# Layer-norm statistics in one block, a planner with other durations, and sums formed by accumulating DMAs, in a gated long-convolution and token-mixing kernel

## The chip, the cores and the metric

The kernel runs on one core of one Trainium2 chip. The metric is the device time of one execution in microseconds (us), as a median of runs; below it stands beside the profile of one further execution, whose span goes from its first to its last instruction. The engines are called PE (matrix), DVE (vector), ACT (scalar), POOL (GpSimd) and SP (which here only issues DMAs).

## The reference, cut to what matters

Inputs are bf16; S is 2048 positions, D is 640 channels, F is 1536. Branch `a` is a causal convolution over the whole sequence, done by Fourier transforms of length 4096; branch `b` is a layer norm followed by an MLP along the sequence (not along the channels); a sigmoid gate per position mixes them.

```
x = A_q
g = sigmoid((x * gate_w).sum(-1, keepdims=True))
# branch a
kv = (4-tap causal shift convolution of A_k) * A_v
y  = irfft(rfft(kv, 2S) * rfft(ssm_k, 2S))[:S] + kv * ssm_D
a  = A_q * y
# branch b
h = layernorm(x)                         # over D
u = gelu(einsum("sd,sf->df", h, w1) + b1)
b = (einsum("df,fs->ds", u, w2) + b2).T
return g * a + (1 - g) * b
```

## The kernel before, in words

Everything of the computation lives in SBUF, 128 partitions wide; the positions are cut into four groups `hk` of 512, each of four tiles `p` of 128, so a tile number is t = 4 hk + p. The stages are these.

- **Loads.** SP issues nearly all of them; `ssm_k`, the rows of A_q into `X`, `k`, `v`, three column chunks of `w1` into two buffers `ring`, then `w2` in four pieces into two buffers `W2` that lie over `ring`.
- **Filter.** PE transposes `ssm_k` (`transp`, tile `wT`), multiplies it with a table of sines `FTB` (`fwd`, groups of four matmuls that ACT evicts into `C`), for two halves h; `mixing` on DVE turns four tile transforms into the spectrum; `v1mix` accumulates by two pairs of POOL DMAs. The filter's spectra are called V0 and V1.
- **Statistics.** `ln_tile` (L840) runs two bn_stats and one bn_aggr per tile on DVE; `ln_apply` (L849), called after every four tiles, forms 1/sqrt(var + eps) on POOL (a sum and a power on four columns) and normalises the four tiles of `X` in place on DVE. POOL also builds `KF`, the taps of the shift convolution, in two large products.
- **Shift convolution and forward transform of kv.** `k_turn` copies `k` into `kp` on DVE and transposes it by DMA into `KT`; `kv` (L897) multiplies with `KF` on PE, ACT evicts `ksh`, DVE multiplies with `v`. Then `fwd` and `mixing` as for the filter give the spectra A0 and A1 (halves of the sequence).
- **First MLP product (m1).** 12 blocks ft of 32 matmuls, X against `ring`, ACT applies gelu into `GT`. Its priority numbers are far above those of the other work, so it fills PE where nothing else is ready.
- **Gate.** DVE multiplies X with `gate_w` into three buffers `gq` that lie over `KF`; ACT sums each (`gsum`, output to `junk`).
- **Second MLP product (m2).** 16 tiles of 24 matmuls in the order of `HORD` (hk = 2, 3, 0, 1), GT against `W2`; ACT evicts into `O1` with bias and gate.
- **Spectral products** on DVE. `cross` (L1038) forms A0 V1 in place of V1, in four halves (two spectra, i = 0 and 1); `y1` (L1045) forms A1 V0 in place of A1 through the scratch `tm[0]` and `tm[1]` and adds `cross`'s result by POOL DMAs (`acc_dma`); `product` does A0 V0. A complex number is held as two blocks of 1280 columns per slot.
- **Inverse.** `invmix` on DVE undoes `mixing` (giving Z1 for the second half of the sequence, Z0 for the first); `inverse` (L1068) runs the inverse transforms on PE with the table `GTB` (DMA transposes of `FTB`), ACT evicts with the gate into one of three buffers `cgb`, DVE multiplies by q (`q_hi` or `q_lo`, loaded a second time) and adds to `O1`, and SP stores the result.

The order of all instructions is made by a planner in the kernel itself, `_Sched.run` (L382): each operation has a duration written down in the code, and a priority that is its number in program order unless one is given; a simulated clock goes forward, and each engine takes the ready operation with the lowest priority number. PSUM is four slots; the MLP may hold two of them and the other products three. The order so found is emitted for each engine, and on the chip each engine and each DMA queue keeps it: an operation whose input is late holds up all that is behind it. The durations are in `dve_dur`, `act_dur`, `mms` and in single calls. A DMA is planned at 0.1 us of issue, its bytes at a rate, and 2 us to landing. `_Tracker` finds the semaphore waits from the memory that each operation reads and writes, so a buffer placed over another (`at=base_of(...)`) brings waits with it.

Nearly all matmuls carry line 293 in the profile, tensor_tensor 617, tensor_scalar 627 and 628, ACT's work 655, copies of k 724, POOL's DMAs 262, SP's 267 and the DMA transposes 260.

Of the kernel before, what the change touches and what calls it, by code (L numbers as in the profile page):

```python
# [322 lines left out]
class _Sched:  # L323
# [58 lines left out]
    def run(self):  # L382
# [29 lines left out]
        while started < n:  # L412
# [6 lines left out]
            for e in engs:  # L419
# [32 lines left out]
                if e in ("SP", "QA") or op.lat < 0:  # L452
# [3 lines left out]
                    op.end = dma_free + 2.0  # L456
# [48 lines left out]
def _build(nc, A_q, A_k, A_v, A_shift_k, A_ssm_k, A_ssm_D, B_x, B_w1, B_b1, B_w2, B_b2, gate_w, out):  # L505
# [10 lines left out]
    with ExitStack() as es:  # L516
# [34 lines left out]
        gwb = alloc("gwb", [128, D], BF16)  # L551
        Drow = alloc("Drow", [1, D], BF16)
        ident = alloc("ident", [128, 128], BF16)
# [7 lines left out]
        vtmp = alloc("vtmp", [128, 16], F32)  # L561
# [21 lines left out]
        gq = [alloc(f"gq{i}", [128, 2, D], BF16, at=base_of(KF) + 2560 * i) for i in range(3)]  # L583
        junk = alloc("junk", [128, D], BF16, at=base_of(KF) + 7680)
# [14 lines left out]
        q_hi = alloc("q_hi", [128, 2, 4, D], BF16, at=base_of(C[0]))  # L599
# [67 lines left out]
        def mms(vt, items, prio=None, name="mm"):  # L667
            dur = sum(max(n_of(r) / 2400.0, 0.06) for _, _, r, _, _ in items)
# [51 lines left out]
        def k_turn(hk):  # L720
# [3 lines left out]
            SC.add("DVE", 0.85, lambda s: T.op("DVE", lambda e: e.tensor_copy(ov, iv), [i[:, :, :]], [o[:, :, :]]), [i[:, :, :]], [o[:, :, :]], prio=0, name="kperm")  # L724
# [115 lines left out]
        def ln_tile(hk, p):  # L840
            t = 4 * hk + p
            xs = X[:, hk, p, :]
            for ci in range(2):
                o, i = stats[:, t, 6 * ci:6 * ci + 6], xs[:, 320 * ci:320 * ci + 320]
                SC.add("DVE", 0.46, (lambda o, i: lambda s: T.op("DVE", lambda e: e.bn_stats(o, i), [i], [o]))(o, i), [i], [o])  # L845
            o, i = mv[:, t, :], stats[:, t, :]
            SC.add("DVE", 0.2, (lambda o, i: lambda s: T.op("DVE", lambda e: e.bn_aggr(o, i), [i], [o]))(o, i), [i], [o])

        def ln_apply(hk):  # L849
            r = slice(4 * hk, 4 * hk + 4)  # L850
            ts("POOL", vtmp[:, r], mv[:, r, 1], 1e-5, None, ALU.add)
            tt("POOL", rstd[:, r], vtmp[:, r], V(cst, 1, [[0, 4]]), ALU.pow)
            for p in range(4):
                t = 4 * hk + p
                ts("DVE", X[:, hk, p, :], X[:, hk, p, :], mv[:, t, 0:1], rstd[:, t:t + 1], ALU.subtract, ALU.mult, mode=4, extra=0.17)

        srcW = lambda h: (lambda kt, p, ci: wT[:, 2 * h + kt, p, 320 * ci:320 * ci + 320])
        for h in range(2):
# [5 lines left out]
            if h == 0:  # L864
                for hk in range(4):
                    for p in range(4):
                        ln_tile(hk, p)
                    ln_apply(hk)
# [63 lines left out]
        for ft in range(FT):  # L932
# [14 lines left out]
            if ft == 0:  # L947
                act(junk[:, :], gwb[:, :], ACT.Copy, acc=gws[:, :], name="gws").after.add(g_)
# [18 lines left out]
        def w2_load(hk):  # L967
            for a in range(2):
                dma(W2[hk % 2][:, 6 * a:6 * a + 6, :], dr(B_w2, a * 6 * 128 * S + 512 * hk, [[S, 128], [128 * S, 6], [1, 512]]), 128 * 6144)

# [3 lines left out]
        HORD = (2, 3, 0, 1)  # L974
        for n_, hk in enumerate(HORD):
            w2_load_at = n_
            W2h = W2[n_ % 2]
            for a in range(2):
                dma(W2h[:, 6 * a:6 * a + 6, :], dr(B_w2, a * 6 * 128 * S + 512 * hk, [[S, 128], [128 * S, 6], [1, 512]]), 128 * 6144)
# [57 lines left out]

        def cross(g):  # L1038
# [114 lines left out]
```

## Time and profile before

| | us |
|---|---|
| median of 3 runs (lowest to highest) | 198.19 (197.91 to 199.74) |
| the profiled execution, its own time | 197.93 |
| its span | 196.1 |
| PE busy | 177.4 |
| DVE busy | 177.0 |
| ACT busy | 118.5 |
| POOL busy | 28.6 |

The mean granted clock of PE was 0.996. In the rows of a timeline, the first number is the start in us from the start of the span, the second the time from the first start to the last end of the merged instructions, then engine, line, operation, output and inputs by the program's names (buffer numbers left out) and their number (x); in brackets stands how long the engine stood idle just before and what ended it. In the rows of groups, the numbers behind the bar are the busy time in us and the mean duration of one in ns, then the idle time before them. Starts of neighbouring instructions overlap a little with the ends of those before, so that the price of one in a row of its kind is read from start to start. PE's ends are modelled.

### The profile page before, as it was taken

The numbers are of one execution on the slowest core, as the hardware profiler recorded it, in microseconds if no ns is written. First come the engines' busy times: TensorE is split into PE (matmuls) and PEld (weight loads), VectorE is DVE, ScalarE is ACT, GpSimd is POOL, SyncE is SP. The second block draws the span as 40 slices with busy tenths as digits, with TensorE's granted clock in tenths as the row PEclk, the third lists the DMA queues.
The fourth block names the chain that finished last, engine by engine and source line by source line (L and its number), as shares of the span: only waits on it lengthen the run. The fifth ranks groups of instructions, "written<-read, shape, count | busy, mean of one in ns | idle before, by whom it ended". The sixth has DMA issues, their size and how long they took to land.

```text
span 196.1 us, 3370 instructions
## 1 busy us (share of the span) xinstructions
PE 177.4 (90%) x1403; PEld 131.4 (67%) x1403; DVE 177.0 (90%) x196; ACT 118.5 (60%) x187; POOL 28.6 (15%) x30
## 2 busy tenths in 40 slices
PE   0759987999999999999999999999999979997890
PEld 0546564468767787777777778888888867775560
DVE  7996998799999179999999879999999599989994
ACT  4798967997749793799796413131313117664471
POOL 2629802500005400000000000040400000000000
PEclk9999999999999999999999999999999999999998
DMA  5999999994999999960053008029999960222034
GB/s 162 331 409 379 364 209 253 310 417 143 165 276 265 227 199 191 258 202 0 3 185 135 3 24 282 15 64 232 234 305 231 383 269 5 91 76 101 3 107 160
DMA packets 36719, 37.62 MB, mean 192 GB/s; under 512 B 15579, under 2 KB 32608, under 8 KB 36704
## 3 DMA queue, kind: packets, MB, share of 16 engines
q1 hardware_dynamic: 34464, 32.15, 54.4%
q0 software_dynamic: 2176, 5.24, 14.4%
q8 instruction: 11, 0.18, 0.4%
q14 instruction: 4, 0.03, 0.0%
q10 hardware_dynamic: 64, 0.01, 0.0%
HBM read 25.87 MB, written 2.62 MB: 145 GB/s over the span
## 4 chain that ended last, share of the span: by engine, by line
PE 67%; DVE 16%; DMA 9%; ACT 3%; POOL 2%; issue 2%; SPq 0%; DVEq 0%
PE pp L293 67%; DMA kn<-in_A_k_dram 5%; DMA X<-in_A_q_dram 4%; DVE kp L724 3%; DVE stats L845 2%; DVE C L617 2%; DVE SS L617 2%; DVE X L628 2%; ACT ksh L655 2%; DVE vkv L617 1%; DVE cgb L617 1%; DVE O L617 1%; POOL rstd L617 1%; POOL vtmp L627 1%; ACT cgb L655 1%
## 5 line engine op out<-in xcount | busy, mean ns | idle before, releaser
L293 PE MATMUL pp<-X,ring 128*128 128x320 bf16 x384 | 55.5, 299 | 1.6 <-DVE X L628 1.6
L617 DVE TENSOR_TENSOR C<-C 128x2560 bf16<-128x2560 bf16 (+1 forms) x28 | 48.9, 1773 | 8.3 <-ACT C L655 5.5
L293 PE MATMUL pp<-GT,W 128*128 128x320 bf16 x384 | 52.8, 299 | 1.1 <-ACT O L655 1.1
L293 PEld LDWEIGHTS pp<-GT,W 128*128 128x128 bf16 x384 | 43.5, 113 | 10.0 <-issue 1.4
L293 PEld LDWEIGHTS pp<-X,ring 128*128 128x128 bf16 x384 | 36.6, 98 | 17.6 <-DVE X L628 2.0
L655 ACT ACTIVATE C<-pp 128x640 bf16<-128x640 f32 x64 | 39.9, 723 | 5.5 <-PE pp L293 5.2
L655 ACT ACTIVATE O<-pp,c,omg 128x640 bf16<-128x640 f32 (+1 forms) x17 | 14.5, 853 | 37.9 <-PE pp L293 37.9
L617 DVE TENSOR_TENSOR tm<-C,C 128x2560 bf16<-128x2560 bf16 (+1 forms) x12 | 22.8, 1930 | 0.0
L262 POOL DMA_DIRECT2D C<-C x6 | 7.5, 1406 | 90.1 <-DVE C L617 90.1
L293 PE MATMUL pp<-wT,FTB 128*128 128x320 bf16 x128 | 20.2, 314 | 0.4 <-ACT wT L655 0.4
L655 ACT ACTIVATE GT<-pp,cc 128x640 bf16<-128x640 f32 x12 | 9.5, 792 | 14.6 <-PE pp L293 14.5
L617 DVE TENSOR_TENSOR C<-tm 128x1280 bf16<-128x1280 bf16 (+1 forms) x16 | 18.0, 1154 | 0.1
L293 PEld LDWEIGHTS pp<-wT,FTB 128*128 128x128 bf16 x128 | 11.9, 102 | 7.8 <-ACT C L655 2.3
L655 ACT ACTIVATE cgb<-pp,gg 128x640 bf16<-128x640 f32 x16 | 12.6, 794 | 6.4 <-PE pp L293 3.3
L293 PE MATMUL pp<-C,GTB 128*128 128x320 bf16 x96 | 13.7, 299 | 2.2 <-DVE C L617 2.2
L293 PE MATMUL pp<-ident,ssm 128*128 128x128 bf16 x80 | 8.4, 265 | 6.2 <-DVE pint L617 5.3
L845 DVE BATCH_NORM_STATS2 stats<-X 128x6 f32<-128x320 bf16 x32 | 13.5, 460 | 0.4 <-DMA X<-in_A_q_dram 0.4
L293 PEld LDWEIGHTS pp<-C,GTB 128*128 128x128 bf16 x96 | 9.2, 98 | 6.4 <-DVE C L617 2.5
L655 ACT ACTIVATE junk<-gq 128x640 bf16<-128x640 bf16 x16 | 11.8, 737 | 0.5
L293 PEld LDWEIGHTS pp<-ident,ssm 128*128 128x128 bf16 x80 | 6.5, 127 | 8.0 <-DMA ssm<-in_A_ssm_k_dram 5.3
L655 ACT ACTIVATE wT<-pp 128x640 bf16<-128x640 f32 x16 | 10.2, 711 | 2.6 <-PE pp L293 2.6
L655 ACT ACTIVATE ksh<-pp 128x1024 bf16<-128x1024 f32 (+1 forms) x12 | 9.6, 893 | 3.2 <-PE pp L293 3.2
(63 smaller groups left out, 176.6 us busy)
## 6 DMA issues: line engine op xcount, KB each, us to landing
ring<-in_B_w_dram SPq DMA_DIRECT2D x12, 512.0 KB, 10.9
W<-in_B_w_dram SPq DMA_DIRECT2D x8, 768.0 KB, 6.9
C<-C POOLq DMA_DIRECT2D x6, 640.0 KB, 11.3
ssm<-in_A_ssm_k_dram SPq DMA_DIRECT2D x4, 640.0 KB, 9.0
X<-in_A_q_dram SPq DMA_DIRECT2D x4, 640.0 KB, 9.3
kn<-in_A_k_dram SPq DMA_DIRECT2D x4, 640.0 KB, 8.5
out_dram<-O SPq DMA_DIRECT2D x7, 320.0 KB, 2.3
vkv<-in_A_v_dram SPq DMA_DIRECT2D x2, 640.0 KB, 4.7
```

The costliest lines, as they stand in the source:

```text
L262: ins = engobj.dma_start(out_ap, in_ap, accum_op=ALU.add, max_dma_last_dim=2560)
L293: ins = self.nc.tensor.matmul(ps_ap, lhsT=lhsT, rhs=rhs, start=start, stop=stop, skip_group_check=True)
L617: return SC.add(eng, d, lambda s: T.op(eng, lambda e: e.tensor_tensor(o, a, b, op), [a, b], [o]), [a, b], [o], prio=prio, name="tt")
L627: return e.tensor_scalar(o, a, s1, None, op0=op0)
L628: return e.tensor_scalar(o, a, s1, s2, op0=op0, op1=op1)
L655: return T.op("ACT", lambda e: e.activation(o, src, func, **kw), rr + [src], ww)
L724: SC.add("DVE", 0.85, lambda s: T.op("DVE", lambda e: e.tensor_copy(ov, iv), [i[:, :, :]], [o[:, :, :]]), [i[:, :, :]], [o[:, :, :]], prio ...
L845: SC.add("DVE", 0.46, (lambda o, i: lambda s: T.op("DVE", lambda e: e.bn_stats(o, i), [i], [o]))(o, i), [i], [o])
```

## The change

1. The planner's durations are altered: DVE 0.04 or 0.08 us of fixed time in place of 0.1 or 0.16, ACT 0.09 + 0.05 per operand in place of 0.19 + 0.09, matmuls 2.5 ns more, bn_stats 0.38 for 0.46, bn_aggr 0.12 for 0.2, the k copy 0.75 for 0.85; a POOL DMA lands 3 us later.
2. `ln_apply` is called once, after all 16 tiles, on 16 columns; POOL also forms the root `sd`, which saves a DVE operation in the gate.
3. `cross`: of the two products that formed A0 V1's first block by a wide product and an add, each is a narrow product now; the second goes to a quarter of `tm[0]` and a POOL DMA adds it.
4. The epilogue of the second half (h = 1) adds to `O1` by a POOL DMA from `cgb`.
5. Memory: `q_hi` lies over `Drow` and `KF` (before over `C[0]`), `gq` over `GTB` (before over `KF`), `junk` is gone.
6. Order in the program: `q_hi` is loaded ahead of the `W2` loads, `q_lo` not before the last of them; the A0 products come behind the first inverse.

```diff
-                    op.end = dma_free + 2.0
+                    op.end = dma_free + 2.0 + (3.0 if e == "POOL" else 0.0)
...
-        gq = [alloc(f"gq{i}", [128, 2, D], BF16, at=base_of(KF) + 2560 * i) for i in range(3)]
-        junk = alloc("junk", [128, D], BF16, at=base_of(KF) + 7680)
+        gq = [alloc(f"gq{i}", [128, 2, D], BF16, at=base_of(GTB) + 2560 * i) for i in range(3)]
...
-        q_hi = alloc("q_hi", [128, 2, 4, D], BF16, at=base_of(C[0]))
+        q_hi = alloc("q_hi", [128, 2, 4, D], BF16, at=base_of(Drow))
...
-            return n / {1: 960.0, 2: 1920.0, 4: 3840.0}[mode] + (0.1 if mode == 4 else 0.16)
+            return n / {1: 960.0, 2: 1920.0, 4: 3840.0}[mode] + (0.04 if mode == 4 else 0.08)
...
-            return n / 1200.0 + 0.19 + 0.09 * nap
+            return n / 1200.0 + 0.09 + 0.05 * nap
...
-            dur = sum(max(n_of(r) / 2400.0, 0.06) for _, _, r, _, _ in items)
+            dur = sum(max(n_of(r) / 2400.0 + 0.0025, 0.056) for _, _, r, _, _ in items)
...
-        def ln_apply(hk):
-            r = slice(4 * hk, 4 * hk + 4)
-            ts("POOL", vtmp[:, r], mv[:, r, 1], 1e-5, None, ALU.add)
-            tt("POOL", rstd[:, r], vtmp[:, r], V(cst, 1, [[0, 4]]), ALU.pow)
-            for p in range(4):
-                t = 4 * hk + p
-                ts("DVE", X[:, hk, p, :], X[:, hk, p, :], mv[:, t, 0:1], rstd[:, t:t + 1], ALU.subtract, ALU.mult, mode=4, extra=0.17)
+        def ln_apply():
+            ts("POOL", sd[:, :], mv[:, :, 1], 1e-5, None, ALU.add)
+            tt("POOL", rstd[:, :], sd[:, :], V(cst, 1, [[0, 16]]), ALU.pow)
+            tt("POOL", sd[:, :], sd[:, :], rstd[:, :], ALU.mult)
+            for t in range(16):
+                xs = X[:, t // 4, t % 4, :]
+                ts("DVE", xs, xs, mv[:, t, 0:1], rstd[:, t:t + 1], ALU.subtract, ALU.mult, mode=4, extra=0.16)
...
-                        act(junk[:, :], gb[:, b, :], ACT.Copy, acc=gacc[:, t:t + 1], name="gsum")
-
-        tt("DVE", gth[:, :], vtmp[:, :], rstd[:, :], ALU.mult, mode=1, prio=0)
-        tt("DVE", gth[:, :], gth[:, :], gacc[:, :], ALU.mult, mode=1, prio=0)
+                        act(gb[:, b, :], gb[:, b, :], ACT.Copy, acc=gacc[:, t:t + 1], name="gsum")
+
+        tt("DVE", gth[:, :], sd[:, :], gacc[:, :], ALU.mult, mode=1, prio=0)
...
         HORD = (2, 3, 0, 1)
+        for kt in range(2):
+            dma(q_hi[:, kt, :, :], dr(A_q, (1024 + 512 * kt) * D, [[4 * D, 128], [1, 4 * D]]), 128 * 5120)
...
         def cross(g):
             for i in range(2):
-                tt("DVE", half(T1, 0), half(A0[g], i), half(V1[g], i), ALU.mult)
-                tt("DVE", half(T1, 1), half(A0[g], i), half(V1[g], i, True), ALU.mult)
-                tt("DVE", comp(V1[g], i, 0), comp(T1, 0, 0), comp(T1, 0, 1), ALU.add)
-                tt("DVE", comp(V1[g], i, 1), comp(T1, 1, 1), comp(T1, 1, 0), ALU.subtract)
+                n_ = ncr[0]
+                ncr[0] += 1
+                tmp = V(tm[0], 1280 * (n_ % 4), [[1, 1280]])
+                tt("DVE", half(T1, n_ % 2), half(A0[g], i), half(V1[g], i, True), ALU.mult)
+                tt("DVE", tmp, comp(A0[g], i, 1), comp(V1[g], i, 1), ALU.mult)
+                tt("DVE", comp(V1[g], i, 0), comp(A0[g], i, 0), comp(V1[g], i, 0), ALU.mult)
+                tt("DVE", comp(V1[g], i, 1), comp(T1, n_ % 2, 1), comp(T1, n_ % 2, 0), ALU.subtract)
+                dma(comp(V1[g], i, 0), tmp, 128 * 5120, stream="POOL", prio=0, accum=True)
...
-                    tt("DVE", ov, cg[:, :, :], ov, ALU.add)
+                    if h == 1:
+                        dma(ov, cg[:, :, :], 128 * 5120, stream="POOL", prio=0, accum=True)
+                    else:
+                        tt("DVE", ov, cg[:, :, :], ov, ALU.add)
...
-        for kt in range(2):
-            dma(q_hi[:, kt, :, :], dr(A_q, (1024 + 512 * kt) * D, [[4 * D, 128], [1, 4 * D]]), 128 * 5120)
-        product(A0[0], A0[0], V0[0])
         Z1 = invmix(A1[0], A1[1], C3a, None, None)
         inverse(1, Z1)
...
         for kt in range(2):
-            dma(q_lo[:, kt, :, :], dr(A_q, 512 * kt * D, [[4 * D, 128], [1, 4 * D]]), 128 * 5120)
+            dma(q_lo[:, kt, :, :], dr(A_q, 512 * kt * D, [[4 * D, 128], [1, 4 * D]]), 128 * 5120).after.add(w2last)
+        product(A0[0], A0[0], V0[0])
         product(A0[1], A0[1], V0[1])
```

More of the change, by code (lines that the diff above doesn't have):

```diff
@@ L551, in _build @@
         gwb = alloc("gwb", [128, D], BF16)
+        ident = alloc("ident", [128, 128], BF16)
         Drow = alloc("Drow", [1, D], BF16)
-        ident = alloc("ident", [128, 128], BF16)
         KF = alloc("KF", [128, NG, 7, 32], BF16)
@@ L560, in _build @@
         rstd = alloc("rstd", [128, 16], F32)
-        vtmp = alloc("vtmp", [128, 16], F32)
+        sd = alloc("sd", [128, 16], F32)
         gpre = alloc("gpre", [128, 16], F32)
@@ L723, in k_turn @@
             iv = V(i, 0, [[32, NG], [D, 4], [1, 32]])
-            SC.add("DVE", 0.85, lambda s: T.op("DVE", lambda e: e.tensor_copy(ov, iv), [i[:, :, :]], [o[:, :, :]]), [i[:, :, :]], [o[:, :, :]], prio=0, name="kperm")
+            SC.add("DVE", 0.75, lambda s: T.op("DVE", lambda e: e.tensor_copy(ov, iv), [i[:, :, :]], [o[:, :, :]]), [i[:, :, :]], [o[:, :, :]], prio=0, name="kperm")
             c0 = 16 + 128 * (hk % 2)
@@ L867, in _build @@
                         ln_tile(hk, p)
-                    ln_apply(hk)
+                ln_apply()
                 for g0 in (0, 10):
@@ L947, in _build @@
             if ft == 0:
-                act(junk[:, :], gwb[:, :], ACT.Copy, acc=gws[:, :], name="gws").after.add(g_)
+                act(gq[2][:, 0, :], gwb[:, :], ACT.Copy, acc=gws[:, :], name="gws").after.add(g_)
             if ft in (1, 3, 5, 7):
```

12 lines of the change are left out of this document (5 added, 7 removed).

## The prediction

> **What bounds the kernel now.** I read the page first, then the timeline of each engine from the first to the last instruction.
>
> ```profile
> span 196.1 us, 3370 instructions
> ...
> PE 177.4 (90%) x1403; PEld 131.4 (67%) x1403; DVE 177.0 (90%) x196; ACT 118.5 (60%) x187; POOL 28.6 (15%) x30
> ...
> PE 67%; DVE 16%; DMA 9%; ACT 3%; POOL 2%; issue 2%; SPq 0%; DVEq 0%
> ```
>
> Two engines are 90% busy and the chain that ends last runs through PE for 67%. So the question is where PE stands still, and who lets it. The timeline of PE:
>
> ```profile
> 23.78 0.99 PE L293 MATMUL pp<-X,ring 128*128 128x320 bf16 x6
> ...
> 27.82 1.00 PE L293 MATMUL pp<-ident,ssm 128*128 128x128 bf16 x15
> ...
> 31.49 1.42 PE L293 MATMUL pp<-X,ring 128*128 128x320 bf16 x8 [0.76 <-DVE X L628]
> ...
> 33.03 5.85 PE L293 MATMUL pp<-wT,FTB 128*128 128x320 bf16 x40
> 39.37 1.43 PE L293 MATMUL pp<-X,ring 128*128 128x320 bf16 x8 [0.49 <-DVE X L628]
> ...
> 91.68 26.24 PE L293 MATMUL pp<-X,ring 128*128 128x320 bf16 x192
> 117.76 39.28 PE L293 MATMUL pp<-GT,W 128*128 128x320 bf16 x288
> 158.11 4.51 PE L293 MATMUL pp<-GT,W 128*128 128x320 bf16 x32 [1.07 <-ACT O L655]
> ...
> 182.28 4.63 PE L293 MATMUL pp<-C,GTB 128*128 128x320 bf16 x32 [2.22 <-DVE C L617]
> ```
>
> The long pieces give the price of a 320-column matmul: 39.28 / 288 = 0.136 us. From about 56 to 157 us PE has no gap, as the chain of waits has it in one piece:
>
> ```profile
> 56.08 100.97 PE pp L293 x782
> ```
>
> Late it waits twice: 1.07 us for a PSUM slot that ACT has not emptied, and 2.22 us for DVE's inverse mixing of the first half (Z0), after which it runs the last inverse. To see what is lost before that, count the work left at 23.78, where the first MLP matmul starts: 384 + 384 MLP, 128 + 128 forward and inverse transforms, 72 of the filter's, 1096 x 0.136 = 149.1 us; the shift convolution, 8.7 us in the row below; 40 filter transposes at 1.00 / 15, 2.7 us.
>
> ```profile
> L293 PE MATMUL pp<-KF,KT 128*128 128x128 bf16 (+1 forms) x160 | 8.7, 213 | 0.0
> ```
>
> That is 160.5 us, so an unbroken PE would end at 184.3. Its last matmul ends at about 191.3 (ACT's last eviction starts at 191.34, below). Of the 7.0 us lost, 3.3 are the two late waits; some 3.7 go between 24 and 56, in waits for normalised X (0.76, 0.49) and in starved stretches such as 40 matmuls in 5.85 us. After PE comes a tail:
>
> ```profile
> 180.09 0.62 ACT L655 ACTIVATE O<-pp,c,omg 128x320 bf16<-128x320 f32 x1 [1.01 <-PE pp L293]
> ...
> 191.34 0.79 ACT L655 ACTIVATE cgb<-pp,gg 128x640 bf16<-128x640 f32 x1 [0.23 <-PE pp L293]
> ...
> 192.17 0.83 DVE L617 TENSOR_TENSOR cgb<-cgb,q_lo 128x1280 bf16<-128x1280 bf16 x1 [0.49 <-ACT cgb L655]
> 193.03 0.96 DVE L617 TENSOR_TENSOR O<-cgb,O 128x640 bf16<-128x640 bf16 x3
> ```
>
> It is 196.1 - 191.3 = 4.8 us: eviction, product with q, adds, and 2.1 us of output DMA.
>
> **The change, part by part. DVE's later half.** The rows:
>
> ```profile
> 69.90 2.83 DVE L617 TENSOR_TENSOR C<-C 128x5120 bf16<-128x5120 bf16 x1 [5.28 <-ACT C L655]
> ...
> 86.14 2.89 DVE L617 TENSOR_TENSOR tm<-C,C 128x2560 bf16<-128x2560 bf16 x2
> 88.94 0.82 DVE L617 TENSOR_TENSOR gq<-X,gwb 128x1280 bf16<-128x1280 bf16 x1
> 89.67 1.56 DVE L617 TENSOR_TENSOR C<-tm 128x1280 bf16<-128x1280 bf16 x2
> 91.15 1.49 DVE L617 TENSOR_TENSOR tm<-C,C 128x2560 bf16<-128x2560 bf16 x1
> ...
> 154.25 1.49 DVE L617 TENSOR_TENSOR C<-C 128x2560 bf16<-128x2560 bf16 x1 [2.57 <-DMA C<-C]
> ...
> 168.57 1.55 DVE L617 TENSOR_TENSOR O<-cgb,O 128x1280 bf16<-128x1280 bf16 x2
> ```
>
> From start to start, a 2560-wide operation costs (88.94 - 86.14) / 2 = 1.40 us and a 1280-wide one (91.15 - 89.67) / 2 = 0.74. A half of `cross` is now two of each, 4.28 us; it becomes one wide and three narrow, 3.62. Four halves save 2.6 us. Four epilogue adds of the second half save 4 x 0.74 = 3.0. The dropped gate operation on 16 columns is 0.1. DVE loses 5.7 us of work ahead of Z0.
>
> Moving `gq` from KF's memory to GTB's lets the eight gate products (8 x 0.73 = 5.8 us) start once the k transposes have read kp1, not after the last shift convolution, which ends at 72.3:
>
> ```profile
> 68.86 3.42 PE L293 MATMUL pp<-KF,KT 128*128 128x128 bf16 x64
> ```
>
> They are ready in DVE's idle 5.28 us before 69.90; they can be what fills it. I count 5 us, between 0 and 5.3.
>
> Against that, `y1` overwrites the whole of tm[0], from which the last `cross` DMA must first have read. Only the 2560 x 2 product into tm[1] can go ahead (2.8 us by the row above), and the subtraction behind the issue (0.74). The trace has no accumulate of 320 KB, only of 640:
>
> ```profile
> L262 POOL DMA_DIRECT2D C<-C x6: 1200/1316/1703, 60.6 to 138.9; - x6
> ...
> DMA to landing us min/median/max: 7.7/11.7/15.3
> ...
> out_dram<-O SPq DMA_DIRECT2D x7, 320.0 KB, 2.3
> ```
>
> Bounds for half that size: 2.3 us (a plain store) and 15.3. I take 7.7, the quickest accumulate, being the same kind of transfer: DVE then waits 7.7 - 2.8 - 0.7 = 4.2 us (0 to 11.8). Its issue costs POOL some 1.3 us, with nothing queued behind but the other accumulates. The 2.57 us wait for A1's accumulate may go or stay; both A0 products are now free to fill it, so no charge. Net, Z0 comes 5.7 + 5.0 - 4.2 = 6.5 us sooner (bounds: 6 us later to 11 sooner). For PE to run through it must come 2.2 us sooner, and 1.6 more for the gains of PE ahead of it that follow; I take the 2.22 us wait as gone.
>
> **What PE gains late.** -2.2 for that wait. The slot wait of 1.07 depends on an order that is made anew; I take half, -0.6 (0 to -1.1). With Z0 early the inverses run before the last MLP tile, since their priority number is lower, and the tail is then an eviction of 320 columns (0.62), one add (0.32 at most, three take 0.96), 2.1 of DMA and a handover: 3.1 us, so -1.7 (0 to -1.7).
>
> **What the accumulating epilogue costs.** Each of three `cgb` buffers stays taken until its DMA has landed, where now the add frees it. The fourth position of the second half reuses the first buffer, so ACT waits in order, with the MLP's evictions queued behind it, and PE behind those. The planner charges 0.1 + 1.0 + 2.0 + 3.0 = 6.1 us from issue to landing and puts other work there; at 7.7 ACT is 1.6 late, which PE's spare slot mostly covers. +1.0 (0 to +9.2).
>
> The Trainium skill, "DMA: Bandwidth & Descriptors", section "Anatomy of one DMA — SWDGE (gpsimd) path", has a GpSimd-issued DMA take about 2.0 us plus its bytes at 436 GB/s, which for 640 KB is 3.5 us; this trace's 7.7 to 15.3 disagree. By the page 320 KB would be an estimated 2.75 us, that cost nothing, and the time 1.0 us lower.
>
> **The front.** Rows of DVE, of the k copies as a group, of POOL and of ACT:
>
> ```profile
> 10.13 0.83 DVE L845 BATCH_NORM_STATS2 stats<-X 128x6 f32<-128x320 bf16 x2
> ...
> 10.99 0.83 DVE L845 BATCH_NORM_STATS2 stats<-X 128x6 f32<-128x320 bf16 x2
> ...
> L724 DVE COPY kp<-kn x4: 815/818/4347, 20.3 to 48.1; 128x2560 bf16<-128x2560 bf16 x4
> ...
> 13.63 3.94 POOL L617 TENSOR_TENSOR KF<-cw,m 128x2240 bf16<-128x2240 bf16 x1 [5.38 <-DVE stats L845]
> ...
> 19.97 4.03 POOL L617 TENSOR_TENSOR KF<-cw,m 128x2240 bf16<-128x2240 bf16 x1
> 29.51 0.23 POOL L627 TENSOR_SCALAR vtmp<-mv 128x4 f32<-128x4 f32 x1 [5.51 <-DVE mv L847]
> 29.82 1.04 POOL L617 TENSOR_TENSOR rstd<-vtmp,cst 128x4 f32<-128x4 f32 x1
> ...
> 30.89 1.51 DVE L628 TENSOR_SCALAR X<-X,mv,rstd 128x640 bf16<-128x640 bf16 x4 [0.62 <-POOL rstd L617]
> ...
> 28.30 3.68 ACT L655 ACTIVATE wT<-pp 128x640 bf16<-128x640 f32 x6 [0.29 <-PE pp L293]
> ```
>
> Now, the first block of X is normalised around 25 us. In one block, 16 tiles x 0.86 us (10.99 - 10.13) from 8.7 end at 22.5, with one kp copy of 0.82 in between at 23.3; then POOL's sum and power on 16 columns. Four columns take 1.04: bounds 1.04 (all fixed) and 4.2 (all per column); I take 0.23 fixed, as the sum beside it takes in all, and the other 0.81 per four columns, 3.5. First block of X: 23.3 + 0.3 + 3.5 + 4 x 0.37 = 28.6 us. Until then PE has only 40 transposes and 8 matmuls, 3.8 us of work in the 4.7 from 23.8, and ACT would hold it there anyway: 8 evictions at 3.68 / 6 = 0.61. So the lost filler costs 0.9 us plus some waiting in order where the plan has the power at 0.33 us. In return the 4.35 us copy at 20.3, which lay beside the second KF product on POOL and ended just after it, shrinks: KF can start at 13.6 and its two pieces run on from there to 21.5, since no rstd now comes between them. And ACT is planned at the 0.62 us it takes instead of 0.72, so fewer MLP groups go in ahead of the filter's transforms. I put the loss in 24 to 56 at 2.7 us where it is now 3.7: -1.0 (-3.5 to +3).
>
> **At nothing.** q_hi now waits for KF (72 us), not for the accumulates that read C[0], and q_lo for the last W2 load; both have until the inverse. If q came late, DVE's product would wait and ACT behind the buffers. The four GTB transposes wait for the gate sums and pass behind the first W2 pair on SP:
>
> ```profile
> L260 SPq DMA_TRANSPOSE GTB<-FTB x4: 2482/3870/6499, 19.9 to 63.4; - x4
> ...
> 98.44 32.92 SPq L267 DMA_DIRECT2D W<-in_B_w_dram  x6
> ```
>
> At 3.9 us of issue each they hold SP 15.5 us; if that begins by 100, the loads of the second pair, free to start at about 117.8, are not touched; if the sums end at 112 as now, they go out 10 us late, against some 13 us for which the first pair feeds PE.
>
> **Sum.** 196.1 - 2.2 - 0.6 - 1.7 + 1.0 - 1.0 = 191.6 us of span. The profiled execution took 197.93, 1.83 outside its span, and the median of the three runs is 198.19, another 0.26: 191.6 + 2.1 = 193.7 us.
>
> **Rivals.** First, PE unbroken: the refitted order loses only the 0.9 us before X; 184.3 + 0.9 + 3.1 + 2.1 = 190.4 us. For it: DVE's Z0 has room. Against: every front wait must vanish at once.
>
> Second, the gain is eaten at the front: the power takes 4.2 us and PE, in order, stands at the first MLP group with the filter's transforms queued behind. Front +3 in place of -1: 197.7 us, no difference that can be told. For it: rstd already gates X on the chain. Against: the present order loses much the same there.
>
> Third, slower: the accumulate's landing in the epilogue. At 15.3 us ACT is 9.2 late; PE has one MLP tile (24 x 0.136 = 3.3 us) in hand and loses 5.9, and if the first half's reuse of the buffers is hit as well, 11.8. In place of +1.0: 198.6 to 204.5, middle 201.5. It decides once the holds cost PE over 5.5 us together: one landing at 14.9, or two at 12.2. For it: the median accumulate takes 11.7. Against: those are twice the size and ran beside the W2 loads.
>
> That the adds leave DVE and nothing happens, because DVE only waits instead, is part of the second.
>
> **How the numbers follow.** Forecast 193.7: 0.54. PE unbroken 190.4: 0.15. Eaten 197.7: 0.18. Slower 201.5: 0.13. One per cent (2 us) is about what these runs can tell from no change. Over 1% faster means below 196.2: nearly all of the first two, 0.67; within 1%, 0.19; slower 0.14. The likeliest case's own range is 191.5 to 196. The range leaves out most of the slower rival and the lowest edge: 189.5 to 199.0.
>
> **What would show it.** Right: PE with no wait for DVE after 150 us, the last matmul before 189 and of the MLP; first normalised X near 27 us and one power of 3 to 4 us; gate products before 75 us; the epilogue accumulates landing in 6 to 9 us. Wrong: ACT waiting on the accumulate at `cgb` for several us with PE waiting for ACT; PE waiting for X over 3 us; the last matmul still an inverse behind DVE; or a W2 wait at the second MLP pair.

## The result, and the profile after

| | before | after |
|---|---|---|
| median in the same comparison, us (lowest to highest) | 198.91 (197.91 to 199.74) | 193.04 (192.91 to 193.10) |
| the profiled execution, us | 197.93 | 193.08 |
| its span, us | 196.1 | 191.3 |
| PE's last matmul ends at, us | 191.3 | 188.2 |

The ratio is 0.9706, with a 95% interval of 0.9649 to 0.9763: 2.9% faster. The forecast was 193.7 us. In the ratios of this document disturbed executions are left out, so that a kernel's median can lie away from its ratio.

Part of the distance between the medians is the clock that PE was granted. Of the 13 executions of the kernel before that were taken beside dve_sums (the first experiment below), seven at a mean clock of 0.995 to 0.998 took 197.99 to 198.86 us and six at 0.987 to 0.989 took 199.44 to 199.82. The kernel after had 0.997 or more in each execution. The two profiled executions, at 0.996 and 1.000, lie 4.85 us apart; the other 1 us of the 5.87 between the medians goes with the lower clock.

First the page of the kernel after: its span, the busy times, and the shares of the chain that ended last.

```profile
span 191.3 us, 3363 instructions
...
PE 177.6 (93%) x1403; PEld 130.8 (68%) x1403; DVE 167.4 (88%) x191; ACT 116.5 (61%) x187; POOL 38.1 (20%) x33
...
PE 74%; DVE 12%; ACT 6%; DMA 3%; POOL 2%; issue 2%; DVEq 0%
```

PE has the same work as before (177.6 us, 177.4 before) in a shorter span. DVE is 9.6 us less busy, ACT 2.0, and POOL 9.5 us more. The chain of waits, from where PE begins to run through:

```profile
51.97 12.86 PE pp L293 x118
64.83 0.03 issue
64.85 123.32 PE pp L293 x928
188.17 0.02 issue
188.19 0.63 ACT O L655
188.82 0.02 issue
188.84 0.33 DVE O L617
```

From 51.97 to 188.17 us PE waits for nobody. Before, the unbroken piece was 56.08 to 157, and two waits (1.07 and 2.22 us) followed. Behind the last matmul stand one narrow eviction, one narrow add and the output DMA: 191.3 - 188.2 = 3.1 us, 4.8 before. The timeline of PE says what ran where:

```profile
25.04 0.44 PE L293 MATMUL pp<-ident,ssm 128*128 128x128 bf16 x5
25.63 3.96 PE L293 MATMUL pp<-ident,ssm 128*128 128x128 bf16 x35 [0.15 <-ACT C L655]
29.72 1.31 PE L293 MATMUL pp<-wT,FTB 128*128 128x320 bf16 x8
30.87 1.40 PE L293 MATMUL pp<-X,ring 128*128 128x320 bf16 x8
...
50.49 0.43 PE L293 MATMUL pp<-vkv,FTB 128*128 128x320 bf16 x2
51.97 3.75 PE L293 MATMUL pp<-vkv,FTB 128*128 128x320 bf16 x26 [1.04 <-DVE vkv L617]
...
150.68 4.58 PE L293 MATMUL pp<-C,GTB 128*128 128x320 bf16 x32
...
176.01 4.54 PE L293 MATMUL pp<-SS,GTB 128*128 128x320 bf16 x32
180.38 7.77 PE L293 MATMUL pp<-GT,W 128*128 128x320 bf16 x56
```

The first inverse starts at 150.68, the last one ends at 180.4, and 56 matmuls of the MLP are still in hand behind it. That is the order that the forecast had asked for. The front is another matter: the transforms of kv (`vkv`) start at 50.49 and wait 1.04 us for DVE's product. DVE and POOL in the front, and DVE where it stood idle for 5.28 us before:

```profile
13.90 7.84 POOL L617 TENSOR_TENSOR KF<-cw,m 128x2240 bf16<-128x2240 bf16 x2 [5.65 <-DVE mv L847]
25.80 1.39 POOL L627 TENSOR_SCALAR sd<-mv 128x16 f32<-128x16 f32 x1 [4.05 <-DVE mv L847]
27.28 2.94 POOL L617 TENSOR_TENSOR rstd<-sd,cst 128x16 f32<-128x16 f32 x1
...
30.25 5.79 DVE L628 TENSOR_SCALAR X<-X,mv,rstd 128x640 bf16<-128x640 bf16 x16 [3.19 <-POOL rstd L617]
...
54.70 0.82 DVE L617 TENSOR_TENSOR gq<-X,gwb 128x1280 bf16<-128x1280 bf16 x1
...
63.78 2.83 DVE L617 TENSOR_TENSOR C<-C 128x5120 bf16<-128x5120 bf16 x1 [1.06 <-ACT C L655]
...
111.77 2.83 DVE L617 TENSOR_TENSOR tm<-C,C 128x5120 bf16<-128x5120 bf16 x1 [1.51 <-DMA C<-tm]
```

One sum and one power on 16 columns (1.39 and 2.94 us) hold X until 30.25. The gate's first product runs at 54.70, and DVE's wait for the transformed kv is 1.06 us, at 63.78 where it was 5.28 at 69.90. The new DMAs by kind, where the last number is the median from issue to landing:

```profile
C<-tm POOLq DMA_DIRECT2D x4, 320.0 KB, 6.1
...
O<-cgb POOLq DMA_DIRECT2D x4, 320.0 KB, 4.2
```

And the issue of the GTB transposes on SP, lowest, median and highest duration in ns and the first and last start:

```profile
L260 SPq DMA_TRANSPOSE GTB<-FTB x4: 1232/1253/1339, 88.0 to 95.7; - x4
```

### The profile page after: what moved, and what is told of

Its sections match the earlier page's. It is cut to its first block, busy times and chain, and to the rows that moved or that the text cites. A ratio compares the mean times of both kernels' runs of the same rounds, so it can differ in the third digit from the quotient of the medians.

```text
span 191.3 us, 3363 instructions
## 1 busy us (share of the span) xinstructions
PE 177.6 (93%) x1403; PEld 130.8 (68%) x1403; DVE 167.4 (88%) x191; ACT 116.5 (61%) x187; POOL 38.1 (20%) x33
## 4 chain that ended last, share of the span: by engine, by line
PE 74%; DVE 12%; ACT 6%; DMA 3%; POOL 2%; issue 2%; DVEq 0%
PE pp L293 74%; DVE X L628 3%; DVE SS L617 3%; DMA ssm<-in_A_ssm_k_dram 3%; DVE C L617 2%; ACT wT L655 2%; ACT C L655 2%; DVE kp L724 2%; POOL rstd L617 2%; DVE vkv L617 1%; ACT FTB L655 1%; POOL sd L627 1%; DVE stats L845 1%; ACT cw L655 0%; ACT O L655 0%
## 5 line engine op out<-in xcount | busy, mean ns | idle before, releaser
L293 PE MATMUL pp<-X,ring 128*128 128x320 bf16 x384 | 53.9, 299 | 0.0
L293 PEld LDWEIGHTS pp<-X,ring 128*128 128x128 bf16 x384 | 37.1, 98 | 15.0 <-DVE X L628 0.5
L617 DVE TENSOR_TENSOR tm<-C,C 128x2560 bf16<-128x2560 bf16 (+2 forms) x12 | 20.2, 1708 | 1.5 <-DMA C<-tm 1.5
L617 DVE TENSOR_TENSOR C<-tm 128x2560 bf16<-128x2560 bf16 (+1 forms) x12 | 15.0, 1264 | 0.1
L262 POOL DMA_DIRECT2D O<-cgb x4 | 4.8, 1200 | 37.2 <-ACT cgb L655 26.7
L655 ACT ACTIVATE gq<-gq 128x640 bf16<-128x640 bf16 x16 | 11.8, 755 | 0.0
L262 POOL DMA_DIRECT2D C<-tm x4 | 3.5, 866 | 40.4 <-DVE C L617 40.4
## 6 DMA issues: line engine op xcount, KB each, us to landing
C<-C POOLq DMA_DIRECT2D x6, 640.0 KB, 10.6
```

What stands on the lines that cost most here:

```text
L262: ins = engobj.dma_start(out_ap, in_ap, accum_op=ALU.add, max_dma_last_dim=2560)
L293: ins = self.nc.tensor.matmul(ps_ap, lhsT=lhsT, rhs=rhs, start=start, stop=stop, skip_group_check=True)
L617: return SC.add(eng, d, lambda s: T.op(eng, lambda e: e.tensor_tensor(o, a, b, op), [a, b], [o]), [a, b], [o], prio=prio, name="tt")
L655: return T.op("ACT", lambda e: e.activation(o, src, func, **kw), rr + [src], ww)
```

## The experiments

The expectations name four theories. P: PE sets the time, and what let it run through is the order that the new durations give. It keeps the forecast's bound, but not the forecast's reason for an early Z0, which was work taken off DVE. D is nearer to that reason: DVE sets the time, and what helped is the work taken off it, by the accumulating DMAs above all. S: the one block of statistics makes the gain. K came later: what counts is where POOL's two `KF` products lie.

**The accumulating DMAs undone (dve_sums).** The kernel after, with the sums of `cross` and of the epilogue on DVE again:

```diff
-                tt("DVE", half(T1, n_ % 2), half(A0[g], i), half(V1[g], i, True), ALU.mult)
-                tt("DVE", tmp, comp(A0[g], i, 1), comp(V1[g], i, 1), ALU.mult)
-                tt("DVE", comp(V1[g], i, 0), comp(A0[g], i, 0), comp(V1[g], i, 0), ALU.mult)
-                tt("DVE", comp(V1[g], i, 1), comp(T1, n_ % 2, 1), comp(T1, n_ % 2, 0), ALU.subtract)
-                dma(comp(V1[g], i, 0), tmp, 128 * 5120, stream="POOL", prio=0, accum=True)
+                tt("DVE", half(T1, 0), half(A0[g], i), half(V1[g], i), ALU.mult)
+                tt("DVE", half(T1, 1), half(A0[g], i), half(V1[g], i, True), ALU.mult)
+                tt("DVE", comp(V1[g], i, 0), comp(T1, 0, 0), comp(T1, 0, 1), ALU.add)
+                tt("DVE", comp(V1[g], i, 1), comp(T1, 1, 1), comp(T1, 1, 0), ALU.subtract)
...
-                    if h == 1:
+                    if h == 2:
```

> The changed kernel with both kinds of accumulating DMA undone: cross and the second half's epilogue add on DVE again. Theory P (PE is the bound; the refitted planner's order makes the gain; DVE has room): DVE gets its 5.7 us of work back and PE still runs without a late gap, 193.0 us within 0.5. Rival D (the work taken off DVE makes the gain, because it brings Z0 sooner): PE waits for DVE again before the last inverse, 195 to 198 us.

Measured: 192.84 us (192.81 to 193.11), ratio 0.9696 (0.9644 to 0.9749). That is the time of the kernel after. PE's end in this kernel:

```profile
173.57 4.51 PE L293 MATMUL pp<-SS,GTB 128*128 128x320 bf16 x32
177.94 9.97 PE L293 MATMUL pp<-GT,W 128*128 128x320 bf16 x72
```

Even with the adds back, the inverse ends before 178.1 us with 72 MLP matmuls in hand. Two of the change's named parts are worth nothing here, and D falls in this form.

**More work for DVE (load1).** The kernel after, in which the second wide product of `product` (into `tm[1]`) is done twice, in each of its four calls:

```diff
         def product(dst, a, v):
             tt("DVE", P2(T0), P2(a), P2(v), ALU.mult)
-            tt("DVE", P2(T1), P2(a), P2(v, True), ALU.mult)
+            for _ in range(2):
+                tt("DVE", P2(T1), P2(a), P2(v, True), ALU.mult)
```

> The changed kernel with 11 us more of DVE work: the wide product into tm[1] is done twice in each of the four spectral products (the same values again, nothing left out). Theory P: PE stays the bound, DVE had some 8 to 10 us of room, and only the end changes, since the plan now has the inverse last (a tail of 4.8 us for 3.1): 194 to 196.5 us. Rival D: DVE is as near the bound as PE, every us counts, 201 to 204 us.

Measured: 195.28 us (195.05 to 195.41), ratio 0.9820 (0.9757 to 0.9883). 11 us more work for DVE cost 2.2. PE's end:

```profile
180.12 3.42 PE L293 MATMUL pp<-GT,W 128*128 128x320 bf16 x24
183.38 4.54 PE L293 MATMUL pp<-SS,GTB 128*128 128x320 bf16 x32
```

PE still runs through, to 187.9; but now the inverse is the last thing, and the tail is 193.2 - 187.9 = 5.3 us in place of 3.1. So DVE's lateness reaches the time first through the tail.

**The durations alone, and all but the durations (new_costs, old_costs).** new_costs is the kernel before with all of the new durations (point 1 of the change) and nothing else; old_costs is the kernel after with the old ones. Cut to two of the eight lines:

```diff
-            return n / 1200.0 + 0.19 + 0.09 * nap
+            return n / 1200.0 + 0.09 + 0.05 * nap
...
-            return n / {1: 960.0, 2: 1920.0, 4: 3840.0}[mode] + (0.1 if mode == 4 else 0.16)
+            return n / {1: 960.0, 2: 1920.0, 4: 3840.0}[mode] + (0.04 if mode == 4 else 0.08)
```

> The kernel before with the planner's new durations alone: statistics in four, all sums on DVE, gate products over KF. Theory P: nearly all of the gain, 191.5 to 194 us. Rivals D and S: 197 to 198.5 us.

> The changed kernel with the planner's durations of before, all else as changed. Theory P: the forward transforms again share PE with more MLP groups, Z0 comes late and the inverse runs last, 196 to 198 us. Rivals D and S: the order matters little, 193 to 194 us.

Measured: new_costs 193.43 us (193.31 to 193.59), ratio 0.9724 (0.9671 to 0.9776). old_costs 197.30 us (196.93 to 198.43), ratio 0.9926 (0.9894 to 0.9957). Beside the median of the kernel before in this comparison, 198.86 us, the numbers written in the planner carry 5.4 us by themselves, and everything else together, without them, 1.6. What old_costs does wrong is seen on PE:

```profile
29.80 1.31 PE L293 MATMUL pp<-wT,FTB 128*128 128x320 bf16 x8
34.02 2.29 PE L293 MATMUL pp<-X,ring 128*128 128x320 bf16 x8 [2.90 <-DVE X L628]
...
182.93 4.53 PE L293 MATMUL pp<-C,GTB 128*128 128x320 bf16 x32
187.30 4.51 PE L293 MATMUL pp<-SS,GTB 128*128 128x320 bf16 x32
```

In its order an MLP group stands ahead of the rest of the filter's transforms, PE stands 2.90 us for X, and the inverse is the last work once more. The wait costs more than its own length, as the page's row of the granted clock shows (40 slices of the span, in tenths of full speed; 9 is 0.9 or more):

```profile
PEclk9999998599999999999999999999999999999999
```

From 34 to 40 us the clock was 0.50. Twenty-four matmuls from 34.02 to 40.19 took 6.2 us, and at 0.136 us each they take 3.3. All ten executions of old_costs had a mean clock of 0.983 to 0.991; from the median, 0.989 of a span of 196 us, the estimate is that 2 us of its time are the clock. With that taken out, and beside the executions of the kernel before at 0.995 or more (median 198.16), the durations alone carry about 4.7 us and everything else without them about 3. The two do not add up to the gain: either by itself removes part of the same loss.

In new_costs DVE's wait for the transformed kv is between the two kernels':

```profile
66.33 2.83 DVE L617 TENSOR_TENSOR C<-C 128x5120 bf16<-128x5120 bf16 x1 [2.40 <-ACT C L655]
```

**Which duration (act_costs, rest_costs).** The kernel before with the line for ACT alone (the first pair of the diff above), and with all of the others but that one.

> The kernel before with one line of the planner altered, ACT's duration (0.09 + 0.05 per operand for 0.19 + 0.09). Theory P, narrowed: it is the 0.1 us too much per ACT eviction that made the planner put MLP groups between the transforms' groups, so this line alone has most of the gain, 193 to 195 us. Rival: no single duration does it, the order improves with all of them, 196 to 198 us.

> The kernel before with all the other new durations (DVE, bn, copies, matmuls, POOL's DMAs), ACT's as before. Theory P, narrowed: little of the gain, 196 to 198.5 us. Rival: DVE's and the statistics' durations matter as much, 193 to 195.5 us.

Measured: act_costs 193.95 us (193.24 to 194.62), ratio 0.9750 (0.9688 to 0.9813). rest_costs 197.22 us (197.05 to 198.94), ratio 0.9944 (0.9905 to 0.9983). One line gives most of it, though two of the four executions of act_costs took 194.6. PE in act_costs:

```profile
48.98 3.42 PE L293 MATMUL pp<-vkv,FTB 128*128 128x320 bf16 x24
...
155.69 3.42 PE L293 MATMUL pp<-GT,W 128*128 128x320 bf16 x24 [1.07 <-ACT O L655]
...
182.22 4.51 PE L293 MATMUL pp<-SS,GTB 128*128 128x320 bf16 x32
```

In the kernel before the first matmul of `vkv` ran at 55.37, behind 80 MLP matmuls; here it runs at 48.98 behind 56, and in rest_costs at 59.58 behind 96. The reading that fits these counts, though the planner's own clock is not on record: with ACT planned at 0.72 us per eviction, the evictions of the transforms pile up in the planner's clock, it fills PE with the MLP, and PE then does that first; with 0.62, as ACT runs, the transforms come through. Z0 follows: the wait for DVE is gone in act_costs, though the slot wait of 1.07 and the long tail (191.5 - 186.7 = 4.8) are still there. The clock fell in rest_costs too (0.50 from 30 to 33 us, behind a wait of 2.42 us for X), but it does not make the difference: two of the ten executions had a clock of 1.000 and took 197.15 and 197.30 us. In rest_costs both of the old DVE waits are still seen, the first longer than before:

```profile
73.75 2.83 DVE L617 TENSOR_TENSOR C<-C 128x5120 bf16<-128x5120 bf16 x1 [8.45 <-ACT C L655]
```

```profile
164.52 4.56 PE L293 MATMUL pp<-C,GTB 128*128 128x320 bf16 x32 [0.87 <-DVE C L617]
```

**Four blocks of statistics (four_stats).** The kernel after with the mean and power taken after every four tiles, as before the change:

```diff
-        def ln_apply():
-            ts("POOL", sd[:, :], mv[:, :, 1], 1e-5, None, ALU.add)
-            tt("POOL", rstd[:, :], sd[:, :], V(cst, 1, [[0, 16]]), ALU.pow)
-            tt("POOL", sd[:, :], sd[:, :], rstd[:, :], ALU.mult)
-            for t in range(16):
+        def ln_apply(hk):
+            r = slice(4 * hk, 4 * hk + 4)
+            ts("POOL", sd[:, r], mv[:, r, 1], 1e-5, None, ALU.add)
+            tt("POOL", rstd[:, r], sd[:, r], V(cst, 1, [[0, 4]]), ALU.pow)
+            tt("POOL", sd[:, r], sd[:, r], rstd[:, r], ALU.mult)
+            for t in range(4 * hk, 4 * hk + 4):
```

> The changed kernel with the statistics in four blocks again (sum, power and root on POOL for four columns at a time). Theory P: the first block of X is normalised some 5 us sooner than the 31.7 us of the changed kernel, PE has MLP work beside the filter's transposes, 191 to 192.5 us. Rival S (one block makes the gain, by taking waits for POOL out of DVE): 194.5 us or more.

Measured: 195.13 us (195.08 to 195.18), ratio 0.9808 (0.9756 to 0.9861). A miss: it is 2.1 us slower than one block, not faster, though X comes 11 us earlier. That is the range of S; but new_costs has four blocks too and took 193.43 us, so the block is not what makes the gain. The timelines of DVE, POOL, ACT and PE in four_stats:

```profile
19.29 6.56 DVE L628 TENSOR_SCALAR X<-X,mv,rstd 128x640 bf16<-128x640 bf16 x8 [0.48 <-POOL rstd L617]
...
20.81 4.14 POOL L617 TENSOR_TENSOR KF<-cw,m 128x2240 bf16<-128x2240 bf16 x1
...
40.06 1.28 ACT L655 ACT_TABLE_LOAD   x1
...
54.81 3.75 PE L293 MATMUL pp<-vkv,FTB 128*128 128x320 bf16 x26 [1.62 <-DVE vkv L617]
```

Eight normalisations take 6.56 us; sixteen took 5.79 in the kernel after, so eight should take 2.9. The group's row (shortest, median and longest, in ns) shows that a single one of them took the whole of the difference:

```profile
L628 DVE TENSOR_SCALAR X<-X,mv,rstd x16: 435/441/4062, 19.3 to 38.4; 128x640 bf16<-128x640 bf16 x16
```

The eight lie over the second product of `KF` on POOL (20.81 to 24.95), which slid behind the rstd of the first two groups. The k copy of 4.35 us in the kernel before lay in the same way over the second `KF` product. And ACT loads the table of the gelu (1.28 us) in the middle of evictions. So there were two suspects for the 2 us, and a run was made for each. By the trace the 2.1 us are made of two pieces: PE ends at 189.4 in place of 188.2, and the tail is 4.0 us in place of 3.1, since only 12 MLP matmuls stand behind the last inverse.

The Trainium skill, "SBUF — State Buffer", section "Who interferes with whom", has DVE's copy and tensor_scalar in their two-port modes and GpSimd lock each other out of a shared pair of ports for a whole instruction. By that rule the normalisations and the second `KF` product cannot overlap in their work, and the trace agrees: 6.56 us is 2.9 plus most of a 4.14 us product, and one instruction of 0.44 us took 4.06.

**The first gelu held back (four_hold).** four_stats, in which the planner places the first gelu behind the last eviction of the first shift convolution:

```diff
+        kve = []
+
         def kv(hk):
...
-                act(o, (lambda s, ng=ng: s[:, 0:128 * ng].rearrange("p (a b c) -> p a b c", a=ng, b=4)), ACT.Copy, vt=vt, name="kve")
+                kve.append(act(o, (lambda s, ng=ng: s[:, 0:128 * ng].rearrange("p (a b c) -> p a b c", a=ng, b=4)), ACT.Copy, vt=vt, name="kve"))
...
             if ft == 0:
+                g_.after.add(kve[5])
```

> The changed kernel with the statistics in four blocks, and with the first gelu held in the plan behind the last eviction of the first shift convolution. Theory: statistics in four came out slower (195.1 us) because the first MLP block is complete sooner and its gelu, with a table load of 1.28 us, falls between the filter's last evictions; with it held back PE's waits of 1.15 us (for ACT) and of 1.62 us (for DVE's product with v) fall by 1 to 1.7 us in sum, 193.4 to 194.2 us. Rival: the four blocks cost it elsewhere (POOL's extra root between the KF products, the end), 194.8 us or more.

Measured: 196.80 us (196.73 to 196.82), ratio 0.9893 (0.9840 to 0.9946). A miss: 1.7 us slower than four_stats. PE, and its granted clock:

```profile
52.73 0.43 PE L293 MATMUL pp<-vkv,FTB 128*128 128x320 bf16 x2 [1.11 <-DVE vkv L617]
54.78 5.38 PE L293 MATMUL pp<-vkv,FTB 128*128 128x320 bf16 x26 [1.62 <-DVE vkv L617]
...
PEclk9999999999969999999999999999999999999999
```

The wait of 1.15 us for ACT is gone from the shift convolution, and PE waits 1.11 us more for DVE's `vkv` instead, which is just as late as in four_stats (54.78 and 54.81). What held `vkv` was DVE, not the table. The 26 matmuls took 5.38 us in place of 3.75 because of the clock: from 54.78 to 60.20 us it was 0.69, and in four_stats it was 1.00 in the same stretch. Those 1.6 us are the whole distance to four_stats, and all four executions had a mean clock of 0.991 (0.996 to 1.000 there). So holding the gelu gained nothing here and by itself lost nothing; the expectation of 193.4 to 194.2 fails either way.

**`KF` first (four_kf).** four_stats, with both `KF` products ahead of all else on POOL:

```diff
-                    tt("POOL", KF[:, g0:g0 + 10, :, :], V(cw, 7 * g0, [[7, 10], [1, 7], [0, 32]]), V(m32, 0, [[0, 10], [0, 7], [1, 32]]), ALU.mult)
+                    tt("POOL", KF[:, g0:g0 + 10, :, :], V(cw, 7 * g0, [[7, 10], [1, 7], [0, 32]]), V(m32, 0, [[0, 10], [0, 7], [1, 32]]), ALU.mult, prio=0)
```

> The changed kernel with the statistics in four blocks and both KF products given first rank on POOL, so that they run on from about 14 to 22 us. Theory K: four blocks cost time because a rstd between the KF pieces puts the second of them beside eight normalisations on DVE, which then took 6.6 us for 2.9; with KF done by then that goes, the product with v comes some 2 to 3 us sooner than in the version with four blocks alone, and the time is 192 to 193.5 us. Rival: KF's place does not matter, 194.5 to 196 us; or X, waiting longer for POOL, is late in turn, over 196 us.

Measured: 191.68 us (191.60 to 192.33), ratio 0.9655 (0.9595 to 0.9715). It is 3.45 us faster than four_stats by one priority. POOL and DVE:

```profile
13.97 7.84 POOL L617 TENSOR_TENSOR KF<-cw,m 128x2240 bf16<-128x2240 bf16 x2 [5.70 <-DVE mv L847]
...
24.93 4.00 DVE L628 TENSOR_SCALAR X<-X,mv,rstd 128x640 bf16<-128x640 bf16 x11
```

Eleven normalisations now take 4.00 us, 0.36 each as in the kernel after. While POOL does `KF`, DVE does bn_stats, two in 0.83 us in all of these kernels. DVE's second product for `vkv` starts at 51.12 in place of 53.27, and PE no longer waits for it. So, as far as these runs go, the one block of the change was good for what it did to POOL's order; with that order made by itself, four blocks are 1.4 us better than one (191.60 to 192.33 us beside 192.91 to 193.10).

That does not make the held normalisation worth 3.45 us by itself. The run new_costs has it too, and the same wait for `vkv`, and took 193.43 us:

```profile
19.31 6.57 DVE L628 TENSOR_SCALAR X<-X,mv,rstd 128x640 bf16<-128x640 bf16 x8 [0.48 <-POOL rstd L617]
...
54.66 3.75 PE L293 MATMUL pp<-vkv,FTB 128*128 128x320 bf16 x26 [1.62 <-DVE vkv L617]
```

What four_stats has beyond new_costs, and loses 1.7 us by, is a wait of 0.60 us for ACT's gelu (PE, 76.91) and the longer tail. The two kernels differ by points 3 to 6 of the change and POOL's root; no run took these apart.

**One block alone (one_block).** The kernel before with only `ln_apply` on 16 columns:

```diff
-                    ln_apply(hk)
+                ln_apply()
```

> The kernel before with the statistics in one block alone (16 columns on POOL, then 16 normalisations), durations and sums as before. Theory K plus P: the front's stall of the k copy goes, but with the old order of the transforms the late waits stay: 196 to 198 us. Rival S: one block carries the gain by itself, 193 to 195 us; or costs by the filler it takes from PE, over 199 us.

Measured: median 200.94 us (198.08 to 202.73), ratio 1.0027 (0.9973 to 1.0080). No gain, where 196 to 198 was expected; the two executions with a clock of 1.000 took 198.08 and 198.15. The profile is of one at 200.66 us. PE:

```profile
34.03 2.29 PE L293 MATMUL pp<-X,ring 128*128 128x320 bf16 x8 [3.06 <-DVE X L628]
...
185.02 4.63 PE L293 MATMUL pp<-C,GTB 128*128 128x320 bf16 x32 [1.82 <-DVE C L617]
```

The first two k copies take 1.50 and 0.81 us where one took 4.35, but with the old durations an MLP group stands ahead on PE, and that waits 3.06 us for X: what the one gives the other takes. Behind that wait the clock of the profiled execution was 0.50 as well (0.52 over 34 to 40 us).

**The parts together (four_kf_dve, four_kf_hold_dve).** four_kf with the sums on DVE as in dve_sums, and that with the first gelu held as in four_hold.

> The same with both kinds of sums on DVE. Theory P: the accumulating DMAs are worth nothing, and the plan ends with MLP tiles, so within 0.7 us of the version before it or a little less: 191.5 to 193 us. Rival D: 1 us or more slower than it.

> The same again with the first gelu held behind the first shift convolution's evictions. If the gelu's table load of 1.28 us costs PE a wait once the product with v is no longer late: 190.8 to 192 us. Rival: DVE still sets when the forward transform starts, no difference to the version before it.

Measured: 191.23 us (190.78 to 191.69), ratio 0.9634 (0.9580 to 0.9687); and 190.58 us (189.90 to 191.00), ratio 0.9597 (0.9543 to 0.9652). The last is faster than both kernels. Its PE:

```profile
51.51 4.01 PE L293 MATMUL pp<-vkv,FTB 128*128 128x320 bf16 x28
...
177.82 7.77 PE L293 MATMUL pp<-GT,W 128*128 128x320 bf16 x56
```

`vkv` finds its input ready, and the last matmul ends at 185.6 us, where the forecast's count has 184.3 for an unbroken PE. Holding the gelu, which lost time while DVE was late, may gain 0.65 us here; the intervals overlap, so that is not certain. That the accumulating DMAs are worth nothing is seen a second time: without them 191.23, with them 191.68.

## Why the prediction was right, point by point

The time (193.04 for 193.7) and the picture of PE hold: PE runs through late, an MLP tile is last, and the tail is short. The reason that the forecast gave for it, work taken off DVE, does not hold, and three terms of the sum were off: the held buffers by 1.0 and the slot wait by 0.5 one way, the front by 1.2 the other. That the sum came within 0.3 us of the span is in part luck. On the span: 196.1 - 2.2 - 1.1 - 1.7 + 0 + 0.2 = 191.3.

- **The wait for Z0, -2.2: right in size, for another reason.** No row of PE after 52 us names DVE. The forecast drew it from 5.7 us of work off DVE and 5.0 us of idle filled by the gate. Neither is needed: dve_sums gives the work back, act_costs keeps it and `gq`'s memory as before, and neither has the wait. What does it lies earlier. In the kernel after, the product that waited 5.28 us at 69.90 waits 1.06 at 63.78, since the transforms of kv come 6 us sooner; ACT's planned duration alone brings them sooner (act_costs). The forecast named this duration, but only as a part of the front's -1.0. Three gate products, 2.2 us, do lie ahead of that wait now.
- **The slot wait, -0.6: it was the whole 1.07.** It is still in act_costs and not in new_costs, so the order decides it.
- **The tail, -1.7: right.** 3.1 us after, by the steps given.
- **The held buffers, +1.0: nothing.** The accumulates of the epilogue land after 4.2 us in the median, inside the 6.1 that the planner charges; the forecast took 7.7 from the quickest one of twice the size. Half the bytes took about half the time. The third rival (201.5) fell with this, and by the profile no wait of ACT names a DMA at `cgb`. By the Trainium skill's sum ("DMA: Bandwidth & Descriptors", "Anatomy of one DMA — SWDGE (gpsimd) path") 2.75 us was the estimate; 4.2 and 6.1 are above it, so the trace disagrees with it again, though it was on the right side.
- **The wait of `tm[0]`, 4.2 us: 1.51.** The landing was quicker than 7.7 us here too (6.1 in the median), and no wait of PE follows from it.
- **The front, -1.0: this is the step that failed; it was +0.2.** By the forecast's own count 188.2 - 184.3 = 3.9 us are lost, 3.7 before. The first block of X was put at 28.6 us; its normalising starts at 30.25 and four of them end at 31.7. The power was near (2.94 for 3.5). Two things came between: DVE did a 1.4 us mixing and a second k copy ahead of the last tile's mean, and POOL's sum took 1.39 us in place of 0.3. It ran from 25.80 to 27.19 beside a DVE tensor_tensor (25.63 to 27.07). What X's lateness costs is shown by the order, not by a wait for X: PE has transforms of the filter to do instead. Of the 3.9 us, 2.0 go where 40 transposes take 4.7 us (25.04 to 29.72) in place of 2.7; the forecast put that down to ACT's eight evictions, and in the trace these run without a break from 25.82 to 30.86 us, but no run tried it. Another 1.2 us stand between the two `vkv` rows: DVE, which stood 3.19 us for the rstd, is late with the product.
- **The k copy shrinks: right.** The row of the copies has 0.81 to 0.82 us for all four. That the whole of DVE is 9.6 us less busy, not 5.7, is mostly these 3.5 us.
- **The GTB transposes, at nothing: right.** They take 1.25 us of issue each and not 3.9, start between 88.0 and 95.7 us, and the next `W2` loads follow at 98.7.
- **The rivals.** The first, an unbroken PE (190.4), holds from 52 us on and fails ahead of it; four_kf_hold_dve, at 190.58, shows that such a time can be reached. The second (gain eaten at the front) describes one_block and old_costs, which keep the old durations, well: 2.9 to 3.1 us of waiting for X, and then 2 to 3 us more by the clock, which this rival did not have. It did not decide here because the durations changed as well.

What stays open: why the granted clock falls behind some waits and not behind others; how much of the 3.45 us of four_kf is the lock between DVE and POOL itself; which of points 3 to 6 costs four_stats its 1.7 us beside new_costs; and what two `cgb` buffers or a longer landing would cost, which wasn't tried.

## What to carry to other kernels

Where a planner written into the kernel makes the order, its durations are the first thing to hold against a trace: 0.1 us too much on one engine's evictions was worth more here than all the work moved off another engine. Before moving work off a 90% busy engine, give it more work in a run: here 11 us more cost 2.2, and the 6 that were taken away brought nothing that the runs could tell. And when a change in blocks or order gives a gain, look for what else moved on the other engines; here the benefit of one block could be had without it, by letting two POOL products come first. And when the same matmuls take longer in one run than in another, read the granted clock of that stretch before looking for a cause in the program.

## What the runs showed of the hardware that was not expected

- The clock granted to PE fell to 0.50 for some 3 to 7 us in four of the traces. PE had stood just before for 2.90 us (old_costs), 3.06 (one_block), 2.42 (rest_costs) and 1.11 and 1.62 (four_hold). The kernel before had a wait of 2.22 us, at 180 us, with a clock of 1.00 behind it. The lower clock cost 1.6 us in four_hold and some 3 in the profiled execution of old_costs.
- A tensor_scalar of 128x640 on DVE takes 0.36 us from start to start, and eight of them 6.56 beside a POOL product of 4.14 us, one of the eight taking 4.06 alone; a copy took 4.35 for 0.82; bn_stats beside the same POOL product is not touched (0.83 us for two).
- It works the other way too: POOL's sum on 128x4 took 1.41 us beside a DVE tensor_tensor (kernel before, at 36.12) and 0.23 us without one (at 29.51); on 128x16 it took 1.39 us beside one.
- An accumulating DMA of 320 KB within the core landed after 4.2 us (epilogue, 155 to 175 us) and 6.1 (`cross`, 83 to 112 us), one of 640 KB after 10.6 (`C` from `C`) or 18.0 (`C` from `SS`), all medians of the kernel after; POOL's time to issue was 0.86 (`cross`) and 1.20 us (epilogue).
- POOL's power of 16 columns takes 2.94 us and of 4 columns 1.04; from these two the estimate is 0.41 fixed and 0.16 a column.
- The table load ahead of the first gelu takes 1.28 us on ACT in each of these traces; the Trainium skill, "ScalarE: Activation LUTs", section "What ACT_TABLE_LOAD costs", has 1283 ns for the load, which agrees.
